# A fused attention and mixture-of-experts kernel: token rows brought in as columns by DMA transposes in place of TensorE transposes, with more rows read early

## The chip, the cores and the metric

The kernel runs on one core of a Trainium2 chip, in one launch. A core has five engines that each follow their own list of instructions: TensorE (PE in the profile; the loading of a stationary operand is shown apart as PEld), VectorE (DVE), ScalarE (ACT), GpSimd (POOL) and SyncE (SP). SP does no arithmetic here; its list holds DMAs. Data moves between device memory and on-chip memory by DMA, issued from SP's, ACT's or POOL's list. The metric is the device time of one execution in microseconds (us), taken as a median over several runs.

## The reference, cut to what matters

```
phi(t) = where(t > 0, t, exp(t) - 1) + 1                     # q, k, v: 8 batches, 8 heads, 576 positions, 64 wide
kv  = phi(k)^T v ;  z = sum_s phi(k)
x   = (phi(q) kv) / (phi(q) z + 1e-6)  -> x: 4608 tokens x 512
noisy = x @ w_gate + log1p(exp(x @ w_noise)) * noise         # 8 experts
top2  = the two experts with the largest noisy value ; g = softmax over these two
for e in 0..7, k in 0..1:   mask = top2[:, k] == e
    out[mask] += g[mask, k] * (relu(x[mask] @ w1[e]) @ w2[e])  # w1: 512 x 1024, w2: 1024 x 512
```

Every token visits two experts. The count of rows per expert depends on the data, about 1,152 on average.

## The kernel before, in words

Matrix operands are bfloat16, sums are float32. The work has three stages that overlap.

**Attention** (`attention`, class `PhaseA`). The eight batches go in four pairs g = 0..3. Loads of q, k and v are issued from POOL. TensorE forms kv, transposes phi(q), and `num` gives the attention output and, through columns appended to kv, the gate logits. The output rows lie in `xr`, of which there are two buffers, so group 3 overwrites group 1's.

**Routing** (`rt_a`, `rt_b`, `rt_c`, `dispatch`). There are five units: groups 0, 1, 2, and group 3 in two parts (units 3 and 4). For each unit VectorE picks the two experts of each token and a row number for each of its two visits. `dispatch` (L391) then scatters the rows to `x_sorted` in device memory: one indirect DMA per 128 tokens and visit (L398), from POOL, followed by a small memset of POOL into a dummy tile (L389). There are 72 such scatters. `x_sorted` has, for each expert, one list of first visits (F, to the expert of lower number) and one of second visits (S). A row is 576 bfloat16 values: 512 of data, and a few fields with the token's number and gates. An expert's F list is cut into `N_F` = 8, 7, 6, 5, 3, 2, 1, 0 tiles of 128 rows and its S list into 8 minus that; what is over goes into a common region of 192 rows, "MID": a tile of 128 and one of 64, collected by two indirect gathers (`mid_gather`, L499). Expert 0 has only F rows and expert 7 only S rows; each is covered by up to 1,216 rows.

**Experts** (`PhaseB`). Rows are handled in blocks of at most 512 (4 tiles) of one expert. For each block the rows are loaded by a plain DMA from SP into `xn`, one row to a partition (`xn_load`, L556). `xn_t` (L577) transposes up to two tiles by four 128x128 TensorE transposes each into a PSUM tile, and ScalarE copies the result to `xt`, the block's rows as columns (four buffers for `xn`, three for `xt`). `mm1` (L622) multiplies by w1 in eight steps of four matmuls and ScalarE applies the relu; `mm2` (L634) multiplies a tile by w2 in eight matmuls, and VectorE scales it by the gate and, for a second visit, adds the partial result `L` of the first. `put` (L655) writes F and MID tiles to `part` with a plain DMA from SP, and S and MID tiles to the output with an indirect scatter from POOL. `gather` (L603) fetches `L` by an indirect gather from POOL. Weights are loaded from POOL (`w_load`, L438), one DMA of 1 MB (as bfloat16) for each of w1 and w2, cast on the way.

**Order.** The order on each engine is written out by hand; each engine runs its list in that order, and each queue of DMAs in the order of issue. A POOL or SP DMA also waits until the eighth DMA before it on the same engine has landed, since eight semaphores are used in turn. `interval` (L677) sets the pattern of the expert stage: two steps of `mm1` for the current block, then one tile of `mm2` of the block before, and so on; the transposes of the next block lie at the two steps "T".

**Early rows.** Some expert work starts before all rows are scattered. `ROUNDS` (L34) says how many F rows of the experts 0 to 2 are certain to be complete after units 0, 1 and 2: after such a unit the running row counter is raised to that bound, so that later units write above it and reads below it need not wait for them. Before: 256 rows after unit 0; 512 and 384 after unit 1; 768, 640 and 512 after unit 2. `attention` and `routing` hold the blocks that use these rows: expert 0 tiles 0-1, 0 tiles 2-3, 1 tiles 0-2, 0 tiles 4-5, 1 tiles 3-4, 2 tiles 0-3. All later blocks (expert 0 tiles 6-9 first, then `PLAN`) need the complete lists.

Of the kernel before, what the change touches and what calls it, by code (L numbers as in the profile page):

```python
# [7 lines left out]
FP32 = mybir.dt.float32  # L8
# [25 lines left out]
ROUNDS = [(0, (256, 0, 0)), (1, (512, 384, 0)), (2, (768, 640, 512))]  # L34
EARLY = 3
# [14 lines left out]
def build_constants(tc, consts, w_gate, w_noise, noise):  # L50
# [23 lines left out]
    c["gap2"] = tile_("gap2", [P, 352])  # L74
# [337 lines left out]
class PhaseB:  # L412


    def __init__(self, ctx, tc, w1, w2, x_sorted, part, out):
        self.tc, self.nc = tc, tc.nc
        self.w1, self.w2, self.x_sorted, self.part, self.out = w1, w2, x_sorted, part, out
        pool = lambda name, bufs: ctx.enter_context(tc.tile_pool(name=name, bufs=bufs, side="left"))
        self.wp = [pool("B_w", 2)]
        self.mp, self.xp, self.hp = pool("B_m", 2), pool("B_x", 3), pool("B_h", 2)  # L420
        self.yp = [pool("B_y", 3)]
        self.lp = self.np = None
        self.ps_h = self.ps_y = self.ps_t = None
        self.count = {}
        self.w, self.m, self.x = {}, {}, {}

        self.left, self.ready = [0] * 6 + [1] * 5 + [2] * 4, set()
# [16 lines left out]
    def meta_load(self, e, kind, i0, nt, group=None):  # L444

        m = self.mp.tile([P, nt, 4], INT32, name=f"meta{nt}{kind}")
        row = self.row(e, kind, i0)
        rows = self.x_sorted[row : row + nt * P, HD // 2 : HD // 2 + 4]
        r = self.nc.sync.dma_start(out=m[:], in_=rows.rearrange("(t p) c -> p t c", p=P))
        self.early(r, group)  # L450
        for i in range(nt):
            self.m[e, kind, i0 + i] = {"gate": m[:, i, 1 : 2] if kind == "F" else m[:, i, 2 : 3]}
        if kind == "S":
            self.raw = m
# [71 lines left out]
    def prepare(self, e):  # L526

        for kind, n in (("F", CAP if e == 0 else N_F[e] * P), ("S", CAP if e == E - 1 else N_S[e] * P)):
            i0 = 0
            while (e, kind, i0) in self.m:  # L530
                i0 += 1
            if n > i0 * P:
                self.meta_load(e, kind, i0, -(-n // P) - i0)
        if 0 < e < E - 1:
            self.mid_gather(e)
# [20 lines left out]
    def xn_load(self, b, group=None):  # L556

        nc, e, t = self.nc, b["e"], 0
        if any(kind != "M" for kind, _ in b["tiles"]):
            b["xn"] = self.np.tile([P, 4, HD], BF16, name="xn") if self.np else self.xp.tile([P, 4, 512], BF16, name="xt")  # L560
        for kind, i0, n in b["parts"]:
            if kind != "M":
                row = self.row(e, kind, i0)
                src = lambda a, z: self.x_sorted[row + a : row + z, 0 : HD // 2].bitcast(BF16)
                k = sum(b["m"][t : t + n]) // P
                r = nc.sync.dma_start(out=b["xn"][:, t : t + k], in_=src(0, k * P).rearrange("(t p) d -> p t d", p=P))
                self.early(r, group)
                if k < n:
                    nc.sync.dma_start(out=b["xn"][0 : P // 2, t + k], in_=src(k * P, k * P + P // 2))
            t += n  # L570

    def xn(self, b, t, dc):
        kind, i = b["tiles"][t]
        x = self.x[b["e"]][:, i, 0 : HD // 2].bitcast(BF16) if kind == "M" else b["xn"][:, t]
        return x[0 : b["m"][t], dc * P : dc * P + P]

    def xn_t(self, b, h):  # L577

        nc = self.nc
        if h == 0:  # L580
            b["xt"] = self.xp.tile([P, 4, 512], BF16, name="xt")
        ts = range(2 * h, min(b["nt"], 2 * h + 2))
        if not len(ts):
            return
        if self.ps_t:
            ps = self.ps_t.tile([P, 2, 4, P], BF16, name="t")[:]
        else:
            ps = _ap(self.ps_y[0].tile([P, 512], FP32, name="b")[:].bitcast(BF16), [[512, 2], [P, 4], [1, P]])
        for i, t in enumerate(ts):
            m = self.rows(b, t)  # L590
            for dc in range(4):
                nc.tensor.transpose(ps[:, i, dc, 0:m], self.xn(b, t, dc), self.c["ident"][0:m, 0:m])  # L592
        for i, t in enumerate(ts):
            m = self.rows(b, t)
            if m == P and i == 0 and len(ts) == 2 and self.rows(b, t + 1) == P:
                nc.scalar.copy(out=b["xt"][:, :, t * P : t * P + 2 * P].rearrange("p c (i r) -> p i c r", i=2), in_=ps)  # L596
                break
            nc.scalar.copy(out=b["xt"][:, :, t * P : t * P + m], in_=ps[:, i, :, 0:m])
# [78 lines left out]
    def interval(self, cur, prev, weights=(), nxt=None):  # L677


        k = prev["nt"] if prev else 0  # L680
        done = half = 0
        for step in [0, 1, "t", 2, 3, "t", "T", 4, 5, "t", "T", 6, 7, "t"]:
            if step == "T":
                if nxt:
                    self.xn_t(nxt, half)
                    half += 1
            elif step == "t":
                if done < k:
                    self.mm2(prev, done)
                    self.put(prev, done)  # L690
                    done += 1
            elif cur:
                self.mm1(cur, step)
        if nxt:
            self.gather(nxt)
        for e, i in weights:
            self.w_load(e, i)
# [59 lines left out]

def attention(pa, pb, c, x_sorted, zrow):
# [12 lines left out]
    nc.vector.memset(zrow[:], 0.0)  # L771

    for e, kind, i, n in ((0, "F", 8, 2 * P), (3, "F", 4, P), (4, "S", 4, P), (7, "S", 8, 2 * P), (E, "S", 0, 1)):
        row = pb.row(e, kind, i)
        for a in range(0, n, P):
            nc.sync.dma_start(out=x_sorted[row + a : row + min(n, a + P), :], in_=zrow[0 : min(P, n - a)])
    nc.sync.dma_start(out=pb.part[NO_P : NO_P + 1].bitcast(INT32)[:, 0 : ROW_W // 2], in_=zrow[0:1])
    nc.sync.dma_start(out=pb.part[NO_P : NO_P + 1].bitcast(INT32)[:, HD - ROW_W // 2 : HD], in_=zrow[0:1])
# [22 lines left out]
    a0, a1 = pb.block(0, ("F", 0, 2)), pb.block(0, ("F", 2, 2))  # L801
    pb.w_tiles(0)
    pb.w_tiles(1)
    for g in range(3):
# [4 lines left out]
        pa.phi(n, "k")  # L809
        if g < 2:  # L810
            pa.load(g + 2, "q")
        if g == 1:
            for i in range(2):
                pa.dispatch(0, 6 + i, 7 + i)
                pb.w_load(0, i)
            pa.dispatch(0, 8, 9)
            pb.xn_load(a0, 0)
            pb.meta_load(0, "F", 0, 2, 0)
# [8 lines left out]
        if g == 2:  # L827
            pa.kv_ev(n, 0)
            pb.xn_t(a0, 0)
            pa.phi(n, "q", 0, 1)  # L830
            pa.kv_ev(n, 1)
        else:
            pa.phi(n, "q", 0, 1)
# [18 lines left out]
        if g == 0:  # L852
            pa.dispatch(0, 0, 6)
        elif g == 1:
            for i in range(2):
                pa.dispatch(1, 3 * i, 3 * i + 3)
                pb.w_load(1, i)
            pa.dispatch(1, 6, 9)
            pb.xn_load(a1, 1)
            pb.meta_load(0, "F", 2, 2, 1)  # L860
            pb.meta_load(1, "F", 0, 3, 1)
        else:
            pa.dispatch(2)
# [14 lines left out]
    pb.xn_t(a1, 0)  # L878
    pb.mm1(a1, *range(8))
    return a1  # L880


def routing(pa, pb, c, first):

    a0, a1 = first, pb.block(1, ("F", 0, 3))
    b0, b1 = pb.block(0, ("F", 4, 2)), pb.block(1, ("F", 3, 2))
    a2, c0 = pb.block(2, ("F", 0, 4)), pb.block(0, ("F", 6, 4))
    pb.w_tiles(2, 1)
    pb.w_tiles(3, 1)
    pb.xn_load(a1, 1)  # L890
    pb.meta_load(0, "F", 4, 2, 2)
    pb.xn_load(b0, 2)
    pb.meta_load(1, "F", 3, 2, 2)
    pb.xn_load(b1, 2)
    pb.meta_load(2, "F", 0, 4, 2)
    pb.xn_load(a2, 2)
    pb.xn_t(a1, 0)
    pa.rt_b(3)
    pb.xn_t(a1, 1)
# [3 lines left out]
    pa.dispatch(3, 0, 3)  # L903
    pb.w_load(2, 0)
    pa.dispatch(3, 3, 6)
    pb.w_load(2, 1)
# [7 lines left out]
    pa.dispatch(4)  # L914
    pb.mids()
    pb.xn_t(b0, 0)
    pb.interval(b0, a1, (), b1)
    pb.prepare(0)
    pb.xn_load(c0)
    pb.interval(b1, b0, (), a2)  # L920
    pb.interval(a2, b1, (), c0)
    return a2, c0
# [7 lines left out]
    3: [[("F", 0, 4)], [("F", 4, 1), ("M", 0, 1), ("S", 0, 1), ("M", 1, 1)], [("S", 1, 2)]],  # L930
# [8 lines left out]
def kernel(  # L939
# [24 lines left out]
    with ExitStack() as order:  # L964
        order.enter_context(tc.manual_schedule())
        right = lambda name, bufs: ctx.enter_context(tc.tile_pool(name=name, bufs=bufs, side="right"))
        with ExitStack() as rout:
# [13 lines left out]
            pb.np = right("B_n", 4)  # L981
# [3 lines left out]
            prev, cur = routing(pa, pb, c, first)  # L985
# [3 lines left out]
        todo = {0: (3, 0), 1: (3, 1)}  # L989
        for e in range(2, E - 2):  # L990
            at = [i for i, b in enumerate(blocks) if b["e"] == e][:2]
            for k, i in enumerate(at):
                todo[i] = (e + 2, k)
        for i, b in enumerate(blocks):
            pb.left += [b["e"]] * sum(kind != "S" for kind, _ in b["tiles"])
        for i, b in enumerate(blocks):
            nxt = blocks[i + 1] if i + 1 < len(blocks) else None
            for nb in blocks[i + 1 : i + 3] if i == 0 else blocks[i + 2 : i + 3]:
# [3 lines left out]
                pb.xn_load(nb)  # L1002
# [4 lines left out]
            if i in todo:  # L1007
                e2, k = todo[i]
                if k == 0 and e2 > 3:
# [36 lines left out]
```

## Time and profile before

| what | value |
|---|---|
| median of 14 runs | 446.77 us (443.09 to 456.27) |
| the profiled execution | 453.54 us, of which the span from first to last instruction 451.7 us |
| PE busy | 370.5 us (82%) |
| POOL busy | 273.5 us (61%) |
| ACT busy | 194.5 us (43%) |
| DVE busy | 185.1 us (41%) |
| TensorE transposes of rows (L592), from `xn`, `xt` and `xm` | 320, some 220 ns each from start to end, pipelined |
| copies of transposed rows by ACT (L596, L598) | 48; 1,012 ns for two tiles, less for smaller ones |
| loads of rows (`xn`), issue to landing | 2.8 to 5.6 us, median 3.5 |
| MID gathers (`xm`), issue to landing | 4.3 to 12.7 us, median 9.4 |
| weight loads, issue to landing | 9.6 to 15.4 us, median 11.2 |
| scatters of rows, issue to landing | 2.4 to 13.2 us, median 3.9 |

Times within the execution are counted from the start of the span. In lists of groups, a row gives line, engine, operation, output and inputs; in a timeline, start, duration, what, and in brackets the idle time before it with what ended it. PEclk is the share of full speed granted to TensorE's clock. [...] TensorE's real rate is read from the starts of neighbouring rows.

### The profile page before, as it was taken

What the parts mean: (1) busy time and instruction counts of PE and PEld (TensorE: products, weight loads), DVE (VectorE), ACT (ScalarE), POOL (GpSimd) and SP (SyncE); (2) the same over time, 40 slices, a digit from 0 to 9 for tenths busy, and PEclk for the clock granted to TensorE, in tenths of its full rate; (3) what the DMA queues carried; (4) which work ended last, traced back from release to release, by engine and by line L of the source; (5) the groups of instructions that cost most, each with busy time, mean ns of one, the idle gap of its engine ahead of it and who ended that gap; (6) DMA issues with size and microseconds to landing.
All of it is one profiled execution on the core that took longest, in us unless ns stands there. A gap on an engine that the chain in (4) does not pass through costs nothing.

```text
span 451.7 us, 7157 instructions
## 1 busy us (share of the span) xinstructions
PE 370.5 (82%) x2641; PEld 220.1 (49%) x2641; DVE 185.1 (41%) x471; ACT 194.5 (43%) x321; POOL 273.5 (61%) x408
## 2 busy tenths in 40 slices
PE   3595577552968699699999999799999799999990
PEld 1384466442735356355565445345645445554550
DVE  2746989997486711112422121311421231331130
ACT  1718653650625335253455443253454335445410
POOL 7120329888888887500185547365848748868781
PEclk9856655587789989999999999699999989999995
DMA  9999996699984499683396999958986995644540
GB/s 129 208 233 208 208 208 163 123 219 226 188 220 169 130 247 257 224 183 117 107 219 207 212 220 195 284 165 175 229 211 202 251 209 182 212 150 146 163 151 29
DMA packets 63010, 85.59 MB, mean 189 GB/s; under 512 B 15887, under 2 KB 45714, under 8 KB 62966
## 3 DMA queue, kind: packets, MB, share of 16 engines
q0 software_dynamic: 36160, 63.91, 64.3%
q1 hardware_dynamic: 25142, 20.96, 15.6%
q10 hardware_dynamic: 1664, 0.18, 0.5%
q8 instruction: 22, 0.36, 0.3%
q14 instruction: 22, 0.18, 0.1%
HBM read 83.88 MB, written 33.79 MB: 260 GB/s over the span
## 4 chain that ended last, share of the span: by engine, by line
PE 49%; DMA 22%; POOL 15%; DVE 6%; issue 3%; ACT 2%; SPq 1%; POOLq 0%; ACTq 0%; DVEq 0%
PE b L645 22%; PE b L630 22%; POOL x_sorted L398 9%; DMA w<-in_moe_w_dram 6%; DMA kq<-in_q_dram 6%; DMA xm<-x_sorted,m_idx 5%; PE t L592 3%; POOL gap L389 2%; DMA x_sorted<-xr,posi 2%; DMA kq<-in_k_dram 2%; ACT e L178 1%; POOL L L613 1%; DMA meta7S<-x_sorted 1%; DVE e L190 1%; DMA xn<-x_sorted 1%
## 5 line engine op out<-in xcount | busy, mean ns | idle before, releaser
L630 PE MATMUL b<-xt,w 128*128 128x256 bf16 (+5 forms) x832 | 153.6, 332 | 4.6 <-ACT xt L596 3.5
L645 PE MATMUL b<-w,hT 128*128 128x512 bf16 (+1 forms) x640 | 148.0, 388 | 0.0
L632 ACT ACTIVATE hT<-b 128x256 bf16<-128x256 f32 (+5 forms) x208 | 98.6, 483 | 104.6 <-PE b L630 102.4
L630 PEld LDWEIGHTS <-w 128*128 128x128 bf16 x832 | 80.9, 101 | 62.1 <-issue 11.9
L645 PEld LDWEIGHTS <-hT 128*128 128x128 bf16 (+1 forms) x640 | 60.0, 101 | 66.8 <-issue 6.3
L398 POOL DMA_INDIRECT x_sorted<-xr,posi x72 | 75.6, 1050 | 23.3 <-issue 11.9
L596 ACT COPY xt<-t 128x1024 bf16<-128x1024 bf16 x30 | 30.4, 1012 | 55.7 <-PE t L592 55.6
L613 POOL DMA_INDIRECT L<-part,mgi x12 | 12.0, 998 | 53.9 <-DMA part<-y 31.6
L178 ACT ACTIVATE e<-kq 128x2304 bf16<-128x2304 bf16 x16 | 33.2, 2120 | 24.0 <-PE misc L209 10.4
L667 POOL DMA_INDIRECT out_dram<-y,si x34 | 33.7, 991 | 15.9 <-DVE y L649 10.3
L613 POOL DMA_INDIRECT L<-part,gi x34 | 34.7, 1020 | 6.9 <-issue 5.4
L209 PEld LDWEIGHTS <-e 64*128 64x128 bf16 x288 | 22.3, 127 | 15.6 <-DVE e L190 11.2
L272 PE MATMUL num<-kvbd,pqt 128*64 128x162 bf16 x288 | 18.5, 301 | 11.3 <-DVE lwt L290 10.6
L592 PE MATMUL t<-ident,xn 128*128 128x128 bf16 (+1 forms) x256 | 20.8, 220 | 7.6 <-DMA xn<-x_sorted 6.5
L209 PE MATMUL b<-v,e 64*128 64x192 bf16 x144 | 20.7, 322 | 7.5 <-DVE e L190 5.2
L592 PEld LDWEIGHTS <-xn 128*128 128x128 bf16 (+1 forms) x256 | 17.3, 99 | 17.0 <-DMA xn<-x_sorted 7.4
L667 POOL DMA_INDIRECT out_dram<-y,msi x12 | 11.7, 976 | 22.4 <-DVE y L649 9.2
L209 PE MATMUL misc<-v,e 64*128 64x192 bf16 x144 | 20.6, 322 | 5.1 <-DMA v<-in_v_dram 5.1
L283 DVE TENSOR_TENSOR xr<-num,rden 128x768 bf16<-128x768 f32 x24 | 21.9, 952 | 3.3 <-DMA x_sorted<-xr,posi 2.6
L272 PEld LDWEIGHTS <-pqt 128*64 128x64 bf16 x288 | 15.4, 147 | 13.9 <-DVE lwt L290 8.1
L190 DVE TENSOR_TENSOR e<-e,kq 128x2304 bf16<-128x2304 bf16 x16 | 21.5, 1358 | 0.3
L651 DVE TENSOR_SCALAR y<-b,meta2F 128x512 f32<-128x512 f32 x14 | 10.4, 749 | 26.3 <-PE b L645 26.2
(170 smaller groups left out, 360.8 us busy)
## 6 DMA issues: line engine op xcount, KB each, us to landing
w<-in_moe_w_dram POOLq DMA_DIRECT2D x16, 1024.0 KB, 11.2
part<-y SPq DMA_DIRECT2D x39, 256.0 KB, 3.9
kq<-in_k_dram POOLq DMA_DIRECT2D x8, 576.0 KB, 9.1
kq<-in_q_dram POOLq DMA_DIRECT2D x8, 576.0 KB, 12.7
v<-in_v_dram POOLq DMA_DIRECT2D x8, 576.0 KB, 25.0
xn<-x_sorted SPq DMA_DIRECT2D x11, 256.0 KB, 3.4
xn<-x_sorted SPq DMA_DIRECT2D x6, 384.0 KB
xn<-x_sorted SPq DMA_DIRECT2D x4, 512.0 KB
```

The costliest lines, as they stand in the source:

```text
L178: self.nc.scalar.activation(out=e, in_=x, func=ACT.Exp)
L190: nc.vector.tensor_tensor(out=e, in0=e, in1=x, op=ALU.min)
L209: nc.tensor.matmul(out=self.kvps[g, h, j][:, KVM * i : KVM * i + KVM], lhsT=e[half, hp, ci, :], rhs=v[half, hp::4, 64 * ci : 64 * ci + 64] ...
L272: nc.tensor.matmul(out=ps[half, hp, KVW * i : KVW * i + KVW], lhsT=self.pqt[g, 3 * t + i][:, hp, half], rhs=self.kvbd[g][:, j, hp, :], sta ...
L398: r = self.nc.gpsimd.indirect_dma_start(out=self.x_sorted, out_offset=bass.IndirectOffsetOnAxis(ap=self.r["posi", u][:, ci - c0, sl : sl + ...
L592: nc.tensor.transpose(ps[:, i, dc, 0:m], self.xn(b, t, dc), self.c["ident"][0:m, 0:m])
L596: nc.scalar.copy(out=b["xt"][:, :, t * P : t * P + 2 * P].rearrange("p c (i r) -> p i c r", i=2), in_=ps)
L613: r = nc.gpsimd.indirect_dma_start(out=L[0:m].bitcast(INT32), out_offset=None, in_=self.part.bitcast(INT32), in_offset=bass.IndirectOffset ...
L630: nc.tensor.matmul(out=ps[:, 0:n], lhsT=w1[:, dc, fc * P : fc * P + P], rhs=b["xt"][:, dc, 0:n], start=(dc == 0), stop=(dc == 3))
L632: nc.scalar.activation(out=b["hT"][:, fc, 0:n], in_=ps[:, 0:n], func=ACT.Relu)
L645: nc.tensor.matmul(out=ps[i * m : i * m + m], lhsT=b["hT"][:, f, t * P : t * P + m], rhs=w2[:, f, :], start=(fc == 0), stop=(fc == 8 // n ...
L667: r = nc.gpsimd.indirect_dma_start(out=self.out, out_offset=bass.IndirectOffsetOnAxis(ap=self.m[e, kind, i]["si"][0:m], axis=0), in_=y[0:m ...
```

## The change: what it does, and the diff

Six things are done together.

1. `xn_load` becomes `x_load`: F and S rows go from `x_sorted` straight into `xt` by a DMA transpose from SP (one for each part of a block). The `xn` tiles, their transposes and the copies are gone. `xt` has four buffers. Only MID tiles are still transposed on TensorE (`mid_t`), at one step "T" for a block.
2. The early rows grow to 2,304 by the bounds after unit 2 (768, 640, 512 and now 384 of expert 3; before 1,920), with 256 rows of expert 2 from unit 1 on. Early blocks after expert 0 tiles 0-3 are: 1 tiles 0-2, 2 tiles 0-1, 0 tiles 4-5, 1 tiles 3-4, 2 tiles 2-3, 3 tiles 0-2.
3. Weights of experts 1, 2 and 3 move: expert 1's from among unit 1's scatters to the start of unit 2's, expert 2's from unit 3's to unit 2's, expert 3's from after the scatters to among unit 4's. Later experts' weights are loaded three experts ahead, not two.
4. The MID rows of expert e+1 are gathered at the first block of expert e.
5. The zero rows that `attention` wrote near its start are written in the loop's first pass (`zeros`).
6. The dummy memset of POOL behind each gather and each output scatter is 416 columns, not 352 (`gap2`); the one behind each row scatter is unchanged.

```
-ROUNDS = [(0, (256, 0, 0)), (1, (512, 384, 0)), (2, (768, 640, 512))]
+ROUNDS = [(0, (256, 0, 0, 0)), (1, (512, 384, 256, 0)), (2, (768, 640, 512, 384))]
-    c["gap2"] = tile_("gap2", [P, 352])
+    c["gap2"] = tile_("gap2", [P, 416])
...
     def prepare(self, e):
-        if 0 < e < E - 1:
-            self.mid_gather(e)
...
+    def x_load(self, b, group=None):
         nc, e, t = self.nc, b["e"], 0
+        b["xt"] = self.xp.tile([P, 4, 512], BF16, name="xt")
         for kind, i0, n in b["parts"]:
             if kind != "M":
+                row, m = self.row(e, kind, i0), sum(b["m"][t : t + n])
+                r = nc.sync.dma_start(out=b["xt"][:, :, t * P : t * P + m],
+                                      in_=self.x_sorted[row : row + m, 0 : HD // 2].bitcast(BF16), transpose=True)
                 self.early(r, group)
             t += n
+    def mid_t(self, b):
+        ts = [t for t, (kind, _) in enumerate(b["tiles"]) if kind == "M"]
+        if not ts:
+            return
+        ps = self.ps_t.tile([P, 2, 4, P], BF16, name="t")
+        (four transposes for each MID tile, then one ACT copy for each)
...
     interval:
-        for step in [0, 1, "t", 2, 3, "t", "T", 4, 5, "t", "T", 6, 7, "t"]:
+        for step in [0, 1, "t", 2, 3, "t", 4, 5, "t", "T", 6, 7, "t"]:
...
     attention, in the loop over g:
+        if g == 0:
+            zeros(pb, x_sorted, zrow)
...
         elif g == 1:
-            for i in range(2):
-                pa.dispatch(1, 3 * i, 3 * i + 3)
-                pb.w_load(1, i)
-            pa.dispatch(1, 6, 9)
-            pb.xn_load(a1, 1)
+            pa.dispatch(1)
+            pb.x_load(a1, 1)
             pb.meta_load(0, "F", 2, 2, 1)
             pb.meta_load(1, "F", 0, 3, 1)
+            pb.x_load(b1, 1)
+            pb.meta_load(2, "F", 0, 2, 1)
+            pb.x_load(b2, 1)
         else:
-            pa.dispatch(2)
+            for i in range(2):
+                pb.w_load(1, i)
+                pa.dispatch(2, i, i + 1)
+            pa.dispatch(2, 2, 5)
...
     routing:
+    pb.w_load(2, 0)
+    pa.dispatch(2, 5, 6)
+    pb.w_load(2, 1)
+    pa.dispatch(2, 6, 9)
...
-    pa.dispatch(3, 0, 3)
-    pb.w_load(2, 0)
-    pa.dispatch(3, 3, 6)
-    pb.w_load(2, 1)
+    pa.dispatch(3)
...
-    pa.dispatch(4)
+    pa.dispatch(4, 0, 1)
+    pb.w_load(3, 0)
+    pa.dispatch(4, 1, 2)
+    pb.w_load(3, 1)
+    pa.dispatch(4, 2, 3)
     pb.mids()
+    pb.meta_load(2, "F", 2, 2, 2)
+    pb.x_load(b2, 2)
+    pb.meta_load(3, "F", 0, 3, 2)
+    pb.x_load(a3, 2)
-    pb.interval(b0, a1, (), b1)
+    pb.interval(a2, a1, (), b0)
+    pb.interval(b0, a2, (), b1)
+    pb.interval(b1, b0, (), b2)
+    pb.interval(b2, b1, (), a3)
     pb.prepare(0)
-    pb.xn_load(c0)
-    pb.interval(b1, b0, (), a2)
-    pb.interval(a2, b1, (), c0)
+    pb.x_load(c0)
+    pb.interval(a3, b2, (), None)
...
-    3: [[("F", 0, 4)], [("F", 4, 1), ("M", 0, 1), ("S", 0, 1), ("M", 1, 1)], [("S", 1, 2)]],
+    3: [[("F", 3, 2)], [("M", 0, 1), ("S", 0, 1), ("M", 1, 1)], [("S", 1, 2)]],
...
     the loop over the later blocks:
-        todo = {0: (3, 0), 1: (3, 1)}
-        for e in range(2, E - 2):
-            at = [i for i, b in enumerate(blocks) if b["e"] == e][:2]
+        todo = {}
+        for e in range(4, E):
+            at = [i for i, b in enumerate(blocks) if b["e"] == e - 3][:2]
-                pb.xn_load(nb)
+                pb.x_load(nb)
+            if (i == 0 or b["e"] != blocks[i - 1]["e"]) and b["e"] + 1 < E - 1:
+                pb.mid_gather(b["e"] + 1)
```

## The prediction

> **What bounds the kernel now.** I read first where each engine is busy by stage (us from start; PE, PEld, DVE, ACT, POOL with instruction counts; PEclk; DMA share; GB/s).
>
> ```profile
> 150.00:165.00 15.00, 9.62 (x58) 5.54 (x58) 7.70 (x53) 6.38 (x16) 13.20 (x22) 0.89 0.71 210
> 180.00:190.00 10.00, 6.58 (x37) 3.07 (x36) 1.62 (x3) 2.39 (x4) 5.42 (x9) 1.00 0.64 206
> 225.00:273.00 48.00, 48.00 (x306) 25.92 (x304) 12.31 (x23) 24.27 (x45) 29.18 (x42) 1.00 0.90 212
> 273.00:287.00 14.00, 11.20 (x76) 6.83 (x75) 1.51 (x5) 3.83 (x10) 6.87 (x10) 0.95 1.00 227
> 400.00:440.00 40.00, 39.90 (x234) 20.04 (x230) 10.22 (x15) 16.29 (x31) 31.08 (x46) 1.00 0.47 148
> ```
>
> Two regimes. Up to about 185 us POOL scatters rows with hardly a pause and TensorE has holes. From 190 to 440 us TensorE is full; the last 11.5 us are the scatters' tail. The chain of waits in order of time (start, duration, what) shows the hand-over and the two places where a full TensorE still stops:
>
> ```profile
> 92.40 14.11 DMA w<-in_moe_w_dram
> 106.78 0.96 POOL x_sorted L398
> ...
> 180.34 4.22 DMA x_sorted<-xr,posi
> 185.33 4.00 DMA xn<-x_sorted
> 190.00 3.25 PE b L630 x8
> ...
> 273.58 12.65 DMA xm<-x_sorted,m_idx
> 286.89 1.71 PE b L630 x8
> ...
> 349.06 10.41 DMA xm<-x_sorted,m_idx
> 359.91 0.87 PE b L630 x8
> ```
>
> So the second regime begins when the last scatter has landed (184.6), and its stops are MID gathers issued behind a weight load in POOL's queue. The timeline of TensorE prices both a transpose group and a stop:
>
> ```profile
> 280.05 0.61 PE L592 MATMUL t<-ident,xn 128*128 128x128 bf16 x8
> 280.49 1.04 PE L630 MATMUL b<-xt,w 128*128 128x256 bf16 x8
> 281.37 1.89 PE L645 MATMUL b<-w,hT 128*128 128x512 bf16 x8
> 283.09 0.39 PE L592 MATMUL t<-ident,xn 128*128 128x128 bf16 x4
> 286.28 0.61 PE L592 MATMUL t<-ident,xm 128*128 128x128 bf16 x4 [2.80 <-DMA xm<-x_sorted,m_idx]
> ```
>
> Eight transposes hold TensorE 0.44 us (280.05 to 280.49), 55 ns each; eight 512-column matmuls hold it 1.72 us. A 128-row tile thus costs 8 x 0.216 for mm2 and as much for mm1: 3.46 us, and the whole expert work is 9,728 rows / 128 = 76 tiles.
>
> **The change, part by part.** *Transposes off TensorE.* From 189 us on 260 L592 matmuls are recorded, 48 of them for MID, which stay: 212 x 55 ns = 11.7 us leave the full engine. ACT loses the copies (mostly 1.0 us), but at 43% busy it isn't the bound: nothing more.
>
> *MID a whole expert ahead.* The stops vanish, with their aftermath: 2.80 us, and after it 1.71 for 0.87, 1.85 for 0.98 and 2.83 for 1.73 us (2.8 in sum, at the reduced clock); at 357 us 2.36 us and 3.37 for 1.73 (1.6). Together 9.6 us. The gathers then have some 33 us (9.5 tiles x 3.46) for their 4 to 13 us. What is late next: VectorE stood 23 us in its list for these rows, so that goes too; gathers of `L` wait for S fields from SP (5.4 us once), without TensorE waiting.
>
> *The scatter phase.* Scatters start every 1.40 us (126.26, 127.66, ...); a weight load takes about 1.0 us of POOL's list. Each load also holds one of eight semaphores for 12.3 us (88.67 to 100.97), or 14.1 us as second of a close pair (92.40 to 106.5), and POOL stops at the eighth DMA behind it:
>
> ```profile
> 100.99 1.60 POOL L398 DMA_INDIRECT x_sorted<-xr,posi  x1 [0.93 <-DMA w<-in_moe_w_dram]
> 106.78 0.96 POOL L398 DMA_INDIRECT x_sorted<-xr,posi  x1 [0.39 <-DMA w<-in_moe_w_dram]
> 173.28 1.00 POOL L398 DMA_INDIRECT x_sorted<-xr,posi  x1 [1.79 <-DMA w<-in_moe_w_dram]
> ```
>
> A scatter behind a load also lands late: the one issued at 96.02 was waited for until 107.5, 11.5 us for a median of 3.9. I walk POOL's new list with these prices. The zero rows leave the loading phase; ACT waited only 1.75 us for the load they disturb, so 1.2 us is gained (0 to 1.75). Unit 1's scatters, without two loads, end at 123.2 (before 126.3). Expert 1's pair goes out at 124.4 and 128.3; its semaphores cost 1.7 and 1.5 us; expert 2's pair goes out at 142.4 and 146.3 (stalls 1.7 and 1.5); unit 2 ends at 156.1, unit 3 at 174.4; expert 3's pair goes out at 178.7 and 182.6, the last scatter at 185.1. Landing behind that pair, it is there at 182.6 + 14.1 = 196.7. Expert 0's tiles 6-9, behind it in SP's list, get their transpose at 197 and are ready at 202 (five for landing), against 189.4 now: +12.6 us.
>
> TensorE has more to do until then. Expert 2's first tiles wait for w1 until 154.7, then 8.6 us; 0's tiles 4-5 need unit 2 (landed 160.4, transposed 165), then three blocks of 6.9 us to 186; expert 3's wait for w1 until 191, plus 8.6: 199.7. Tiles done when tiles 6-9 begin: 15, and mm1 of three more, 16.5; before 11, and mm1 of four more, 13. 3.5 tiles x 3.46 = 12.1 us ahead. The phase nets +0.5. Its range is wide: -5 if scatters overtake the weights, +10 if transposes and three close pairs slow each other.
>
> *DMA transposes.* No row shows one. Nearest is SP's queue, plain loads among small and large packets:
>
> ```profile
> q0 software_dynamic: 36160, 63.91, 64.3%
> q1 hardware_dynamic: 25142, 20.96, 15.6%
> ```
>
> Its packet takes 15.6% x 16 x 451.7 / 25,142 = 45 ns, so a row of 1 KB some 45 ns of one of 16 engines. If a transpose is as quick, 512 rows move in 1.4 us; if each row goes in four pieces (a tile is 128 columns wide) at a whole packet's price, in 5.8 us. Over 8,576 rows the upper end is 8,576 x 3 x 45 / 16 = 72 us more of all engines, 16% of the span, beside a share of 0.47 to 1.00 now. A block's transpose is issued two intervals before use (about 2 x 12 us), so either is hidden, with the later landings bounded by 0 and +10. I take +1: nearer the plain load, since bytes are the same.
>
> [...]
>
> *POOL's memsets.* 192 columns take 275 ns and 352 take 410, so 416 take about 464: 54 ns x 103 = 5.6 us. Cover: POOL is busy 31.1 of the 40 us from 400; there it gains 23 x 0.054 and has about 36 us left: 90%. Uncovered it would be 5.6; I take +1.
>
> Sum: +0.5 - 11.7 - 9.6 + 1 + 1 = -18.8 us. On the profiled execution: span 451.7 - 18.8 = 432.9, plus the 1.8 around it 434.7 for 453.5. That execution lies 6.8 above the median; on the median 446.8 - 18.8 = 428.
>
> **The rivals.**
>
> *The scatter phase eats half.* The three load pairs, now side by side with transposes, take longer; w1 of experts 2 and 3 and the last landing come later. For it: DMA share above 1 in early slices; against it: the work ahead of tiles 6-9 is 18 tiles, not 15. At +9 us: 437.
>
> *No change to be measured.* That, and in addition the last experts turn POOL-bound: experts 5 to 7 need 58 gathers and scatters at 1.64 us = 95 us of POOL, against about 28.5 tiles x 3.46 = 99 of TensorE. With +9 and the uncovered memsets at 5.6 and a DMA loss near 4, 446.
>
> *Slower: transposes are serial.* If the chip takes 128x128 pieces one after another, SP's transposes become the bound. [...] It decides above 1.18 us a piece (128 + 65 x 4 x 1.18 + 16.5 = 451); below about 1.1 the early start hides it. [...] Against it: plain loads of 256 KB on this queue land in 3.4 us, 77 GB/s, where one engine at 45 ns for 1 KB would give 23, so such DMAs are spread over many engines.
>
> **How the numbers follow.** About the forecast (420 to 434) 0.58; scatter phase eats half (434 to 444.5) 0.20; within 0.5% 0.05; serial transposes or another slow form (449 to 485) 0.17. A measurement of this kernel can tell about 0.5%, 2.2 us. Faster 0.78, same 0.05, slower 0.17. The range 417 to 449 leaves out the slow case and 0.03 of the first. The likeliest case alone is 420 to 434.
>
> **What would show it.** After: no L592 rows but MID's 48; TensorE without MID stops in 200 to 420 us; tiles 6-9 of expert 0 starting near 202; the last scatter landing near 197 behind expert 3's weights; transposes landing within 10 us. Wrong, if `xt` ends TensorE's idle time in the expert stage (serial transposes), if tiles 6-9 start beyond 210 (the scatter phase), if PE waits for `part` rows or buffers while POOL is full near the end (memsets), or if weights land in 20 us and not 12 (contention).

## The result, and the profile after

The changed kernel takes 441.57 us (median of 10 runs, 436.72 to 447.68) against 447.4 us for the kernel before: ratio 0.9858, 95% interval 0.9821 to 0.9895, so 6.3 us faster (4.7 to 8.0). The forecast was 428.0, 18.8 us faster. The direction and the wide range held; two thirds of the gain did not come.

The profiled execution took 445.87 us with a span of 444.1. It and a second profile lie some 4 us above the median, so stops read from them are a little large; sums against runs are made with medians. Busy time by stage (us from the start; PE, PEld, DVE, ACT, POOL with counts; PEclk; DMA share; GB/s), kernel after:

```profile
180.00:190.00 10.00, 10.00 (x70) 6.66 (x69) 2.71 (x4) 3.95 (x11) 5.91 (x9) 1.00 1.05 251
190.00:206.00 16.00, 10.48 (x61) 5.68 (x60) 1.83 (x4) 5.35 (x12) 4.84 (x7) 0.92 0.90 207
225.00:273.00 48.00, 48.00 (x312) 27.63 (x311) 15.59 (x36) 19.91 (x48) 29.88 (x40) 1.00 0.91 186
273.00:287.00 14.00, 9.47 (x67) 5.60 (x66) 2.07 (x9) 4.49 (x12) 7.27 (x10) 1.00 1.19 248
328.00:360.00 32.00, 28.48 (x149) 14.31 (x148) 5.66 (x14) 10.13 (x21) 22.66 (x31) 0.95 1.15 213
400.00:440.00 40.00, 31.34 (x169) 15.36 (x167) 9.00 (x12) 10.36 (x21) 31.64 (x43) 0.95 0.43 137
```

From 180 to 190 us TensorE is now full, where it was busy 6.6 of 10 us: the early rows fill the hole. But the hole has only moved, to 190-206; and in 273-287 TensorE works 9.5 of 14 us where it worked 11.2, though the MID stop in it is gone. The DMA engines' share there has risen from 1.00 to 1.19 (the share adds up the packets' times, so above 1 they overlap). The chain of waits (start, duration, what) says what TensorE stands for:

```profile
124.20 2.49 DMA x_sorted<-xr,posi
126.97 14.32 DMA xt<-x_sorted
...
199.85 5.50 DMA xt<-x_sorted
205.40 3.17 PE b L611 x8
...
260.73 15.55 DMA xt<-x_sorted
...
283.15 16.27 DMA xt<-x_sorted
...
316.12 20.63 DMA xt<-x_sorted
336.80 3.17 PE b L611 x8
...
433.50 0.97 POOL out_dram L648
435.10 0.91 POOL out_dram L648
```

The long transfers in this chain from 126 us on are all DMA transposes, where before they were weight loads, a row load and MID gathers. (The eight matmuls behind two of the stops take 3.17 us, where the eight of the same width at 299.46 below take 1.69: PEclk is 0.50 from 203.6 to 210.2 us and from 336.7 to 339.9, and 1.00 from 299 to 302.) The timeline of TensorE gives the stops of the expert stage in its brackets, 10.0 us in sum:

```profile
276.32 1.05 PE L611 MATMUL b<-xt,w 128*128 128x256 bf16 x8 [2.65 <-DMA xt<-x_sorted]
286.63 1.89 PE L611 MATMUL b<-xt,w 128*128 128x512 bf16 x8 [1.88 <-DMA xt<-x_sorted]
299.46 1.69 PE L611 MATMUL b<-xt,w 128*128 128x448 bf16 x8 [1.99 <-DMA xt<-x_sorted]
336.80 3.17 PE L611 MATMUL b<-xt,w 128*128 128x448 bf16 x8 [3.52 <-DMA xt<-x_sorted]
```

SP's list shows a second effect. Rows are start and duration in SP's queue. The issue of a transpose takes 1.7 us in the median, but some hold the list for 13 (12.8 the longest single one), and the puts and transposes behind them wait:

```profile
269.17 12.77 SPq L561 DMA_TRANSPOSE xt<-x_sorted  x1
282.05 1.01 SPq L642 DMA_DIRECT2D part<-y  x2
283.15 1.95 SPq L561 DMA_TRANSPOSE xt<-x_sorted  x1
...
300.42 13.33 SPq L561 DMA_TRANSPOSE xt<-x_sorted  x2
...
334.78 13.00 SPq L561 DMA_TRANSPOSE xt<-x_sorted  x2
```

The list of DMA queues and issues (packets, MB, share of 16 engines; then median us to landing):

```profile
q1 hardware_dynamic: 51366, 20.96, 24.4%
...
xt<-x_sorted SPq DMA_TRANSPOSE x30, 14.3
```

SP's queue moves the same 20.96 MB in 51,366 packets where it needed 25,142. In the trace's DMA records a plain row is one packet of 1,024 bytes; a transposed row is four of 256. And a transpose lands in 14.3 us (median of the nine of 30 whose landing the trace tells, 3.2 to 17.4), where a plain load took 3.5 in the kernel before (eight of 29).

### The profile page after: what moved, and what is told of

Same layout as the page of the kernel before. It is cut to its first block, busy times and chain, and to the rows that moved or that the text cites. A ratio compares the mean times of both kernels' runs of the same rounds, so it can differ in the third digit from the quotient of the medians.

```text
span 444.1 us, 6741 instructions
## 1 busy us (share of the span) xinstructions
PE 353.8 (80%) x2433; PEld 210.0 (47%) x2433; DVE 184.7 (42%) x474; ACT 166.6 (38%) x301; POOL 280.5 (63%) x408
## 3 DMA queue, kind: packets, MB, share of 16 engines
q1 hardware_dynamic: 51366, 20.96, 24.4%
## 4 chain that ended last, share of the span: by engine, by line
PE 52%; DMA 22%; POOL 14%; DVE 6%; issue 3%; ACT 2%; POOLq 0%; SPq 0%; DVEq 0%; ACTq 0%
PE b L611 24%; PE b L626 24%; DMA xt<-x_sorted 17%; POOL x_sorted L398 9%; DMA v<-in_v_dram 4%; POOL gap L389 2%; POOL out_dram L648 1%; PE misc L209 1%; PE b L209 1%; DVE e L190 1%; POOL kq L163 1%; ACT e L178 1%; DVE xr L283 1%; DVE kq L187 1%; DMA x_sorted<-xr,posi 1%
## 5 line engine op out<-in xcount | busy, mean ns | idle before, releaser
L613 ACT ACTIVATE hT<-b 128x256 bf16<-128x256 f32 (+5 forms) x224 | 102.3, 461 | 193.4 <-PE b L611 190.2
L611 PEld LDWEIGHTS <-w 128*128 128x128 bf16 x896 | 88.4, 101 | 94.1 <-issue 24.2
L398 POOL DMA_INDIRECT x_sorted<-xr,posi x72 | 75.8, 1053 | 25.7 <-issue 12.2
L632 DVE TENSOR_SCALAR y<-b,early 128x512 f32<-128x512 f32 x18 | 13.5, 750 | 33.8 <-PE b L626 33.5
L504 POOL DMA_INDIRECT xm<-x_sorted,m_idx x12 | 12.4, 1032 | 17.5 <-DMA x_sorted<-xr,posi 13.3
L272 PEld LDWEIGHTS <-pqt 128*64 128x64 bf16 x288 | 15.6, 148 | 13.6 <-DVE lwt L290 8.1
L601 POOL MEMSET gap<- 128x416 f32 x46 | 21.2, 461 | 0.1
L656 POOL MEMSET gap<- 128x416 f32 x45 | 20.9, 465 | 0.0
L389 POOL MEMSET gap<- 128x192 f32 x72 | 20.9, 290 | 0.0
## 6 DMA issues: line engine op xcount, KB each, us to landing
v<-in_v_dram POOLq DMA_DIRECT2D x8, 576.0 KB, 11.6
```

Source lines behind the costliest of these rows:

```text
L272: nc.tensor.matmul(out=ps[half, hp, KVW * i : KVW * i + KVW], lhsT=self.pqt[g, 3 * t + i][:, hp, half], rhs=self.kvbd[g][:, j, hp, :], sta ...
L389: self.nc.gpsimd.memset(self.c["gap"], 0.0)
L398: r = self.nc.gpsimd.indirect_dma_start(out=self.x_sorted, out_offset=bass.IndirectOffsetOnAxis(ap=self.r["posi", u][:, ci - c0, sl : sl + ...
L611: nc.tensor.matmul(out=ps[:, 0:n], lhsT=w1[:, dc, fc * P : fc * P + P], rhs=b["xt"][:, dc, 0:n], start=(dc == 0), stop=(dc == 3))
L613: nc.scalar.activation(out=b["hT"][:, fc, 0:n], in_=ps[:, 0:n], func=ACT.Relu)
```

## The experiments

Theory A: the four packets per row are the cause; each takes its turn beside a weight packet. Theory B: the rows are late because SP's list is held by the `y` rows that it puts. Ratios are to the kernel before, with 95% intervals.

**1. Plain loads again, all else as changed.**

```
-                r = nc.sync.dma_start(out=b["xt"][...], in_=self.x_sorted[row : row + m, ...], transpose=True)
+                r = nc.sync.dma_start(out=b["xn"][:, t : t + k], in_=src(0, k * P).rearrange("(t p) d -> p t d", p=P))
...
     def xn_t(self, b, h):        # TensorE transposes and ACT copies at both steps "T", as before
```

> The changed kernel with its DMA transposes undone: every block's rows come by plain loads (1 KB packets) and TensorE transposes them, as before; the early rows, the lists' rounds and MID an expert ahead stay. Theory A (a DMA transpose of rows goes in 256-byte packets, four times as many, each taking its turn beside a weight packet, so it lands late): the waits of TensorE for `xt` at 170, 276, 287, 299 and 337 us (1.6 + 2.7 + 1.9 + 2.0 + 3.5) and the slow-clock stretches behind two of them (4.2) vanish, tiles 6-9 of expert 0 start 2 us earlier, and 212 transposes at 55 ns (11.7) come back: 441.6 - 11.6 - 4.2 - 2 + 11.7 = 435.5, between 433 and 439. Theory B (the rows are late because SP's list is held by the `y` rows that it puts, and by VectorE's waits for `L`): the waits for rows stay, and 11.7 us are added: about 453.

Measured: 442.25 us, ratio 0.9876 (0.9805 to 0.9947). Against the changed kernel's 0.9858 that is a difference of 0.8 us, give or take 3.6: the DMA transposes as such are worth about nothing. The time lies above the range that A gave and far below B's 453. The trace bears out A and not B: in the expert stage TensorE waits for no rows (25.00 of 25.00 us busy in five of the six 25 us windows from 250 to 400), though the puts stand in SP's list as before. The plain loads land later than in the kernel before (median 6.2 us, of the 16 of 32 that the trace tells), but still in time. The number that A gave was too low for a reason of its own: it took stops read in an execution 4.3 us above the median off the median; made against that execution it is 439.8, for 441.2 in the profile of this kernel. The chain of waits of this kernel shows a limit that comes next:

```profile
391.17 3.47 DMA part<-y
395.54 1.05 POOL L L642
397.21 1.03 POOL L L642
...
428.13 0.97 POOL out_dram L696
429.73 0.91 POOL out_dram L696
```

From the last `part` rows of expert 6 on, POOL issues 22 gathers and scatters, one every 1.63 us, which is 36 us. TensorE is full as long, so the two end together (last `y` at 428.4 us, last scatter at 429.7): what more TensorE saves after 391 us would be lost.

**2. No weight loads for experts 4 to 7** (these experts use the weights of experts 0 to 3).

```
-                if k == 0:
-                    pb.w_tiles(e2, {4: 1, 5: 2}.get(e2, 0))
-                parts = [(e2, k)]
+                pb.w[e2] = pb.w[e2 - 4]
```

> The changed kernel without the weight loads of experts 4 to 7, which use the weights of experts 0 to 3 (so the output of these experts is another). DMA transposes as in the changed kernel. Theory A (turns with weight packets): every transpose after 210 us lands in 2 to 4 us instead of 10 to 20, SP's list isn't held by their issue, and the four waits of TensorE for `xt` from 276 to 337 us (10.0) with 1.7 to 3.3 of slow clock behind them vanish: 429 to 430. Theory B (SP's list is held by puts of `y`): the transposes still land late and the time is within 2 us of 441.6. If the transposition itself were slow (a fixed 10 us and more for 256 rows), also no change.

Measured: 437.4 us, ratio 0.9774 (0.9697 to 0.9851): some 4 us under the changed kernel, give or take 4, a third of what A said. The windows, though, show the waits for rows gone, as A had it; compare with 273-287 and 328-360 above:

```profile
275.00:300.00 25.00, 25.00 (x137) 12.34 (x136) 5.70 (x8) 10.32 (x20) 18.24 (x26) 1.00 0.74 198
325.00:350.00 25.00, 25.00 (x142) 13.12 (x141) 7.87 (x18) 8.51 (x18) 19.39 (x27) 1.00 0.67 180
```

From the first `mm1` of expert 0's tiles 6-9 to the last `y` it takes 204.98 to 417.03 = 212.1 us; in the changed kernel 205.40 to 432.16 = 226.8. Some of it is lost again behind the last scatter: from its issue to the end of the span there are 15.4 us here and 9.0 there. SP's queue waits at the end of the program for TensorE's queue, 8.4 us here (first row, longest) and 3.5 in the changed kernel:

```profile
SPq L1033 <- PEq L1033: 9.0, 2, 8.4
```

Why TensorE's queue arrives later there stays open.

**3. Four packets per row, without a transposition.** As experiment 1, but each 128-row tile is loaded so that its rows lie in four separate pieces.

```
+                for a in range(t, t + k):
+                    r = nc.sync.dma_start(out=b["xn"][:, :, a * P : a * P + P],
+                                          in_=src(...).rearrange("p (c d) -> p c d", c=4))
```

> As the kernel with plain loads and TensorE transposes, but each row of 1 KB is loaded in four packets of 256 bytes (one load for each tile of 128 rows), which is how the DMA transposes' packets look, without a transposition. Theory A (the count of packets beside weight packets decides): loads beside weight loads land in 8 us and more, where plain loads of 1 KB take 3 to 4, and the time is 8 to 15 us above the plain kernel's. Rival (the transposition in the DMA is what is slow, not its packets): loads land in 3 to 5 us and the time is within 3 us of the plain kernel's.

Measured: 444.41 us, ratio 0.9934 (0.9901 to 0.9967), 2.6 us above experiment 1 by the ratios, give or take 3.5. As a time that is the rival's number and not A's 8 to 15. The DMA records, though, answer the question of the landing itself, and for A. Two loads of 256 rows each, the same two in four kernels: one while POOL's queue is idle (near 220 us of the span), one at some 260 us, where a weight load is under way unless it was taken out. The last two columns count the packets of 256 bytes and more that SP's and POOL's queues moved in the time of that second load, with the mean time of POOL's:

| kernel | packets of the load | queue idle | at 260 us | SP's packets then | POOL's packets then |
|---|---|---|---|---|---|
| plain loads | 256 of 1,024 B | 1.4 us | 4.0 us | 384 | 186, mean 206 ns |
| pieces, no transposition | 1,024 of 256 B | 1.7 us | 11.6 us | 1,174 | 1,272, mean 128 ns |
| DMA transposes | 1,024 of 256 B | 1.5 us | 10.3 us | 1,053 | 1,091, mean 136 ns |
| DMA transposes, no weight loads | 1,024 of 256 B | 1.4 us | 2.3 us (no weights) | - | - |

With small packets, POOL's queue moved about one packet for each of SP's, weights of 1 or 2 KB against rows of 256 bytes. Over 16 engines POOL's packets alone fill 1,272 x 128 ns / 16 = 10.2 of the 11.6 us, and 1,091 x 136 / 16 = 9.3 of the 10.3. In the plain load's 4.0 us they fill 2.4. So the transposition costs nothing here (10.3 us with it, 11.6 without); the landing goes with the packets. How the DMA engines choose between the queues no run shows. The 256 KB of the load came at 25 and 23 GB/s in packets of 256 bytes (10.3 and 11.6 us), and at 66 in packets of 1,024 (4.0 us). Why the time rose so little is argued and not shown: here the longest issue in SP's list is 5.1 us, with transposes 12.8, so loads and puts behind it are less late, and TensorE's two longest waits for rows in the expert stage are 1.7 and 1.0 us. In the changed kernel both the late landing and the held list do harm. The transpose that TensorE waits for at 299.46 was issued at 283.15, right behind the issue of 12.77 us; in experiment 1 the same rows were asked for 10 us earlier (SP's list there):

```profile
273.34 0.56 SPq L576 DMA_DIRECT2D xn<-x_sorted  x1
```

What each is worth in the time was not separated.

**4. Transposes three blocks ahead.**

```
             (the loop two blocks ahead keeps prepare() alone)
+            for nb in blocks[i + 1 : i + 4] if i == 0 else blocks[i + 3 : i + 4]:
                 pb.x_load(nb)
...
+            pb.xp2 = [right("B_x2", 3)]                         # seven buffers for xt
```

> The changed kernel with each DMA transpose from expert 1's second block on issued three blocks ahead of its use, not two (7 buffers for `xt`, not 4). Theory A (a transpose lands late because its packets take turns with weight packets): 7 to 14 us more lead cover landings of 14 to 20 us, so most of the 10 us of waits after 210 us go: 432 to 435. But where POOL's chain of gathers and scatters from 391 us on sets the end, as in the kernel with plain loads, the last 2 us of it are lost again. Theory B (SP's list is held by puts of `y`): a transpose that stands behind fewer puts is issued earlier too, so B gives no other number here.

Measured: 435.23 us (433.51 to 436.69), ratio 0.9739 (0.9686 to 0.9791). At the upper end of what A said, and better than both kernels: 5 us under the changed kernel by the ratios. The second profile of the changed kernel ran beside it:

> The changed kernel unaltered, beside the others on one chip, for a second profile: the first lay 4.3 us above the median of its runs. Both theories: 441 to 442. If the waits of TensorE for `xt` cost what the first profile shows, they are there again (276, 287, 299 and 337 us, 10 us in sum); the slow-clock stretches behind them should be smaller by about the 4 us.

Measured: 444.42 us in six runs, ratio 0.9837 (0.9764 to 0.9909); waits for `xt` at 274 and 299 us are there again (3.64 and 3.90 us), those at 287 and 337 are not (none above 0.9 us). In the kernel with three blocks' lead no wait for `xt` of 0.9 us or more is left after 210 us. The timeline of TensorE shows what stays, and the chain of waits the road to the last row:

```profile
203.68 3.17 PE L611 MATMUL b<-xt,w 128*128 128x448 bf16 x8 [5.05 <-DMA xt<-x_sorted]
...
289.19 2.46 PE L626 MATMUL b<-w,hT 128*128 128x512 bf16 x8 [2.25 <-DVE y L630]
```

```profile
270.88 12.17 DMA part<-y
...
283.89 4.39 DMA L<-part,mgi
...
388.03 2.43 DMA part<-y
391.35 1.05 POOL L L594
```

A put of `y` that lands 12 us late delays a gather of `L`, that delays VectorE, and TensorE stands 2.25 us for a free bank. The end is POOL's again from 388 us on, but now the last scatter follows the last `y` by 1.8 us (423.78, 425.56); in the second profile of the changed kernel by 5.0 us (430.01, 434.99), since POOL had fallen behind.

**5. DMA transposes only for experts 6 and 7**, else as experiment 1.

```
+def by_dma(b):
+    return b["e"] >= 6
```

> The kernel with plain loads everywhere, but DMA transposes for the lists of experts 6 and 7, whose rows arrive when no weight load is under way any more. Theory A: these transposes land in 2 to 5 us and are hidden; TensorE loses 18 tiles x 4 x 55 ns = 4 us of transposes, of which as much shows as POOL's chain at the end lets: 1 to 4 us under the plain kernel's 442.3. Rival (a DMA transpose is slow by itself): TensorE waits for `xt` in experts 6 and 7 and the time is above the plain kernel's.

Measured: 437.11 us (436.36 to 437.71), ratio 0.9798 (0.9748 to 0.9849): 3.5 us under experiment 1 by the ratios, as A gave, though the intervals overlap. After 200 us TensorE has no wait of 0.9 us or more for rows. So DMA transposes where no weights move are hidden.

**6. MID an expert ahead, alone, in the kernel before.**

```
-        if 0 < e < E - 1:
-            self.mid_gather(e)
...
+            if (i == 0 or b["e"] != blocks[i - 1]["e"]) and b["e"] + 1 < E - 1:
+                pb.mid_gather(b["e"] + 1)
```

> The kernel before with one part of the change: MID rows gathered a whole expert ahead. By the prediction's step both stops with their slow-clock stretches go: 9.6 us, 447.4 - 9.6 = 437.8, ratio 0.979. If the gathers only move the stop to another place (the scatter that they are now ahead of, or a later weight load's semaphore): less than 4 us.

Measured: 442.87 us, ratio 0.9873 (0.9801 to 0.9946): 5.7 us (2.4 to 8.9), not 9.6. Both stops are gone. To see what had been counted too much, the kernel before was profiled again:

> The kernel before, unaltered, for a second profile: the first lay 6.8 us above the median of its runs, and the forecast took its MID stops (2.80 and 2.36 us) and the slow-clock stretches behind them (4.4 us) from it. If the stretches belong to the stops, they are there again; if they belong to that one execution, the stops stand alone and MID an expert ahead is worth 5.2 us and not 9.6, as the 5.7 us of the kernel with MID ahead alone suggest.

Measured: a single run of 466.15 us, on a chip where the kernel before takes 461.7 us; only its stops are read. Timeline of TensorE, kernel before, second profile:

```profile
301.92 0.40 PE L592 MATMUL t<-ident,xm 128*128 128x128 bf16 x4 [3.26 <-DMA xm<-x_sorted,m_idx]
302.15 1.04 PE L630 MATMUL b<-xt,w 128*128 128x256 bf16 x8
...
372.50 0.61 PE L592 MATMUL t<-ident,xm 128*128 128x128 bf16 x4 [2.61 <-DMA xm<-x_sorted,m_idx]
```

Both stops are there (3.26 and 2.61 us; before 2.80 and 2.36), but the eight matmuls behind the first take 1.04 us where the first profile had 1.91: no slow clock. PEclk is 1.00 from 300 to 312 us, where the first profile had 0.50 from 285.7 to 292.3 around the same place, and 0.57 in 372 to 376 (first profile 0.50 from 360.8 to 364.0). So both stops repeat. The slow stretch behind the first (2.8 of the 9.6 us) came in one execution and not in the other; that behind the second (1.6 us) came in both. And the other way round, in the changed kernel:

```
-            if (i == 0 or b["e"] != blocks[i - 1]["e"]) and b["e"] + 1 < E - 1:
-                pb.mid_gather(b["e"] + 1)
...
     def prepare(self, e):
+        if 0 < e < E - 1:
+            self.mid_gather(e)
```

> The changed kernel with one part undone: MID rows are gathered where they were before, when an expert is prepared, and not an expert ahead. By the forecast's step 9.6 us are lost: 451. By what MID ahead alone gave in the kernel before, 5 to 6: 447. If the waits for `xt` cover the MID stops (both fall behind the same weight loads, so TensorE would stand anyway), 0 to 3: 442 to 444.

Measured: ratio 0.982 (0.970 to 0.994), 449.9 us on that slower chip. Set against 0.9858 this is no loss, give or take 5.8 us: 9.6 is excluded, and a loss beyond 4 us is unlikely. In the profile TensorE stops once for MID, 10.62 us at 293 us, and only once (1.99 us) for `xt` after 210 us. That fits the third expectation, that one kind of stop covers the other, but the interval is too wide to show it.

**7. Expert 3's weights earlier, and 352 columns again**, on experiment 4.

```
-    pa.dispatch(3)
+    for i in range(2):
+        pa.dispatch(3, i, i + 1)
+        pb.w_load(3, i)
+    pa.dispatch(3, 2, 6)
...
-    pa.dispatch(4, 0, 1)
-    pb.w_load(3, 0)
-    pa.dispatch(4, 1, 2)
-    pb.w_load(3, 1)
-    pa.dispatch(4, 2, 3)
+    pa.dispatch(4)
...
-    c["gap2"] = tile_("gap2", [P, 416])
+    c["gap2"] = tile_("gap2", [P, 352])
```

> As the kernel with transposes three blocks ahead, with two more edits: the weights of expert 3 are loaded behind the first two columns of scatters of unit 3 and not amid those of unit 4, so that the last scatters don't land behind 2 MB of weights, and POOL's spacing memsets are back at 352 columns. The last scatter should then land near 190 and not 199, and tiles 6-9 of expert 0 start when TensorE has done what is ahead of them, near 200 and not 205: 5 us, and 1 to 2 from the memsets if POOL sets the end: 425 to 429. If expert 3's w1 then holds up expert 2's or the puts instead, no gain.

Measured: 438.58 us, ratio 0.9829 (0.9786 to 0.9871): a miss, slower than experiment 4. The last scatters have landed by 190.9 us, as expected, and the wait before tiles 6-9 is gone, but a longer one appears in its place (timeline of TensorE):

```profile
177.37 1.89 PE L611 MATMUL b<-xt,w 128*128 128x256 bf16 x8 [10.95 <-DMA xt<-x_sorted]
```

The weights, issued at 160.6 and 164.3 us, now move beside transposes of the routing stage issued at 163.0 and 167.4: the delay has moved with them.

**8. Tiles 6-9 of expert 0 ahead of expert 3's first tiles**, loaded plainly, with expert 3's weights behind the last scatter, on experiment 4.

```
+    pa.dispatch(4)
+    pb.w_load(3, 0)
+    pb.w_load(3, 1)
...
+    pb.interval(b2, b1, (), c0)
+    pb.interval(c0, b2, (), a3)
```

> As the kernel with transposes three blocks ahead (435.2), with expert 0's tiles 6-9 worked before expert 3's first tiles and not after them, loaded plainly and transposed by TensorE, and with expert 3's weights loaded behind the last scatter and not before it. In the kernel with transposes three blocks ahead, TensorE stands 5.1 us before tiles 6-9 and works 3 us longer behind it at the slow clock, because the last scatter lands behind 2 MB of weights and the transpose beside them. With the swap the last scatter should land near 187, tiles 6-9 be ready near 192 when TensorE comes to them, and w1 of expert 3 be there near 199, before they are done: 428 to 432. If the plain load beside expert 3's weights lands as late as a transpose (8 us and more), no gain.

> The kernel with transposes three blocks ahead and the swap of expert 0's tiles 6-9 with expert 3's first tiles, unaltered, on another chip, since the executions of the last three runs were disturbed (the kernel before took 461.7 us there). If the wait of 5.1 us before tiles 6-9 and the 3 us of slow clock behind it are gone: ratio 0.957 to 0.966 (428 to 432). If w1 of expert 3 or the plain load beside it is late instead: 0.972 and above, as without the swap.

Measured on two chips where the kernel before takes 461.7 and 464.6 us: ratio 0.9686 (0.957 to 0.980), then 0.9707 (0.962 to 0.979). The intervals hold the value without the swap, 0.9739. In the second profile the plain load is issued at 197.6 us, lands 9.9 us later beside expert 3's weights, and TensorE waits 4.9 us for it: the second expectation. No gain is shown.

## Why the prediction was wrong, point by point

- **Transposes off TensorE, -11.7 us, with +1 for the DMA transposes: the +1 is the step that failed.** The transposes did leave TensorE (only MID's 48 are left). But changed kernel against plain loads gives -0.8 = -11.7 + x, so x = 10.9 us and not 1, give or take 3.6. That is the upper of the prediction's two bounds, "hidden or +10". The x takes it that the 11.7 us come through whole, and no run shows that: with three blocks' lead 6.1 us, give or take 4, separate the transposes from plain loads. Two sentences of the prediction fell. "Nearer the plain load, since bytes are the same": beside weights about one packet of POOL's queue, 136 ns in the mean, went for each of SP's (1,091 and 1,053), so the same bytes took 10.3 us in small packets and 4.0 in large ones. The 45 ns a packet, multiplied by four, priced the queue as if it had the engines to itself; it was also a mean over all packets of that queue, of which those of 1 KB took 56 ns. "A block's transpose is issued two intervals before use (about 2 x 12 us)": many blocks have two tiles, some 7 us and not 12. In the chain above issue to use was 15.6, 16.3 and 20.7 us; less the stops, TensorE came for the rows after 12.9, 14.3 and 17.2 us, and the median landing was 14.3. With a third block's lead the waits for rows in the expert stage went. The sign "if `xt` ends TensorE's idle time in the expert stage" was met, but it had been put down to serial transposes.
- **What is late next.** The prediction gave the landings a range but passed over SP's list and put no term to the weights. A transpose's issue holds SP's list for up to 13 us, and with it the puts of `y`, and POOL's gathers of `L` wait for those (9.29 us at 303.09, below). And the delay goes both ways: two weight loads land late too (some 23 and 17 us, below), which the prediction had named as a sign ("if weights land in 20 us and not 12"). POOL's timeline, kernel after:

```profile
287.83 0.97 POOL L442 DMA_DIRECT2D w<-in_moe_w_dram  x1
...
303.09 1.06 POOL L594 DMA_INDIRECT L<-part,mgi  x1 [9.29 <-DMA part<-y]
...
311.20 0.99 POOL L648 DMA_INDIRECT out_dram<-y,si  x1 [1.65 <-DMA w<-in_moe_w_dram]
...
319.10 0.87 POOL L442 DMA_DIRECT2D w<-in_moe_w_dram  x1
...
336.60 0.92 POOL L648 DMA_INDIRECT out_dram<-y,msi  x1 [5.55 <-DMA w<-in_moe_w_dram]
```

  The DMAs at 311.20 and 336.60 are the eighth behind a weight load, which thus took some 23 and 17 us; in experiment 1 the same two took 14.0 and 11.7. In the second profile of the changed kernel they took 24.4 and 17.7. There POOL doesn't catch up (from 373 us on its list runs without a pause), and 5 us lie between the last `y` and the last scatter.
- **MID, -9.6: mechanism right, size off.** Measured alone -5.7 (-8.9 to -2.4). The stops were 5.2 us; of the 4.4 us of slow clock behind them, 2.8 did not come again in a second execution, but were taken as if every run had them. In the changed kernel undoing this part cost nothing that could be measured.
- **The scatter phase, +0.5: about right.** The walk of POOL's list held: expert 3's pair went out at 179.0 and 182.8 (forecast 178.7 and 182.6), the last scatter at 185.5 (185.1). POOL's timeline, kernel after:

```profile
179.04 0.82 POOL L442 DMA_DIRECT2D w<-in_moe_w_dram  x1
...
182.76 0.96 POOL L442 DMA_DIRECT2D w<-in_moe_w_dram  x1
...
185.47 0.97 POOL L398 DMA_INDIRECT x_sorted<-xr,posi  x1 [0.17 <-issue]
200.06 1.05 POOL L504 DMA_INDIRECT xm<-x_sorted,m_idx  x1 [13.34 <-DMA x_sorted<-xr,posi]
```

  POOL saw that scatter landed at 200 us (forecast 196.7), and tiles 6-9 started at 205.4 and, in the second profile, 203.1 (forecast 202). MID ahead alone (0.9873) and everything but the DMA transposes (0.9876) take the same time: early rows, moved weights, zeros and memsets net nothing, within some 4.5 us. (The zeros gave 0.2 of the 1.2 us put down for them: the first scatter starts at 64.65 us, before 64.83. The walk's other errors made up for it.)
- **Memsets, +1: price right, worth not isolated.** They take 461 and 465 ns, 464 forecast; 22 of them lie in POOL's last chain in experiment 1, by which the estimate is 22 x 54 ns = 1.2 us. No run changes them alone. The rival's premise, a POOL-bound end, is half true: in experiments 1 and 4 POOL's chain ends the program, level with TensorE.
- **Rivals.** Serial transposes are excluded: 256 rows are eight 128x128 pieces in 1.5 us, 0.19 us each, where 1.18 was the point of decision (65 of the 67 tiles one after another from 128 us on, and 16.5 us for the last block and the tail). On a quiet queue a transpose was about as fast as a plain load (1.5 us against 1.4, and 256 KB in 1.5 us are 175 GB/s), beside weights it was not (10.3 against 4.0). The half-eaten gain (434 to 444.5) is where the time fell, but by another way than the scatter phase.

With x and MID as measured and the other terms as forecast the sum is +0.5 - 11.7 + 10.9 - 5.7 + 1 = -5.0 us, against the measured -6.3 (-8.0 to -4.7). It is no independent proof: x was itself taken from the changed kernel's time, and MID's worth from the kernel before.

## What to carry to other kernels

Price a DMA beside a loaded queue by its number of packets, and not by its bytes alone: here rows in packets of 256 bytes went with about one packet of the loaded queue each (1,053 with 1,091, 1,174 with 1,272), in packets of 1,024 bytes with half of one (384 with 186). A form that cuts rows in four was 2.6 to 2.9 times as late here (10.3 and 11.6 us against 4.0), and needs its lead or a place without that traffic; the traffic beside it was late too (weight loads of 23 and 17 us against 14.0 and 11.7). Ask also how long its issue holds the list it stands in (here up to 12.8 us). Take from a profile that lies above the median only the stops that a second profile repeats.

## What the runs showed of the hardware

- A DMA transpose of bfloat16 rows of 1 KB went in packets of 256 bytes. Alone, 256 rows took 1.5 us, a plain load 1.4; beside a weight load 10.3 and 4.0; in these 10.3 us POOL's queue moved 1,091 packets and SP's 1,053, in the 4.0 us 186 and 384.
- A transpose's issue held SP's list 1.2 us at least, where a plain load's median was 0.54, and up to 12.8 us beside weight loads.
- Beside transposes two weight loads of 1 MB took some 23 and 17 us, beside plain loads 14.0 and 11.7.
- With a stop of TensorE of 2.80 us PEclk fell to 0.50 for 6.8 us (kernel before, from 285.6 us), and for 3.4 us with one of 2.36 (kernel before, from 360.7), one of 3.52 (kernel after, from 336.6) and one of 2.25 (experiment 4, read from PEclk 0.93 over 275 to 300). It stayed at 1.00 with one of 2.65 us (kernel after), and with one of 3.26 at the same place in the program as that of 2.80 (kernel before, second profile).
